# Sums of second-layer weights in the last block pair: held in program order, moved to other places, and split 512 wide

## The chip, the cores and the metric

The kernel runs on one core of a Trainium2 chip. The metric is device time in microseconds, the median of several runs of the whole kernel. A core has five engines with instruction queues of their own: TensorE (PE, matmuls, with PEld for its weight loads), VectorE (DVE), ScalarE (ACT), GpSimd (POOL) and SyncE (SP, which here only issues DMAs). An engine works through its queue in order, so an instruction that waits holds up all that stand behind it.

## The reference: block attention, then a mixture of four experts

```python
def _attn_ref(q, k, v):                  # q, k, v: (4, 8, 768, 64)
    k_sum = max over blocks of 32 keys;  v_sum = mean over blocks of 32
    scores_l = scale * q @ k.T, masked to |i - j| < 16
    scores_s = scale * q @ k_sum.T + log(32)
    a = softmax over [scores_l, scores_s]
    return a @ [v, v_sum]

def _moe_ref(x, domain_probs, w1, w2):   # x: (3072, 512), E = 4, F = 1024
    p = domain_probs / (domain_probs.sum(-1, keepdims=True) + 1e-09)
    for e in range(E):
        h = np.maximum(x @ w1[e], 0.0)
        out += p[:, e:e + 1] * (h @ w2[e])
```

The attention is abridged here to its formulas. Its output, turned to 3072 rows of 512, is the x of the experts. Inputs and output are float32; the kernel carries each operand of a large product as two parts, a high part and the rest (low), and forms three products of them.

## The kernel before: staging, order and the names that matter

The 3072 rows are eight blocks of 384. Block 0 and block 1 and then both together are run through two experts each in float32 parts; the other six blocks are run as three pairs (1, 2, 3 in `PAIRS`, line 928), all four experts for a pair, in float16 parts. Pair 3 takes the experts in the order 3, 2, 1, 0. The attention of later blocks is interleaved with the experts' products of earlier ones; it is done when pair 2 is.

**The products.** In a pair the first product (x with w1, `first`, line 1174) multiplies 2 x 2 blocks with seven block products in place of eight, so it needs sums and differences of the blocks of x and of w1. `SEVEN` (line 1034) lists the seven steps m = 0 to 6: the PSUM bank (a, b, c, d) that a step adds to, and its two operands. Some steps are followed by a copy or a sum from bank to bank: at m = 0 ACT copies a to b, at m = 1 it copies d into a tile called `five`, at m = 2 DVE forms c from b and `five`, at m = 4 it forms d from b and `five`. In the traces the banks of the first product are pha to phd, those of the second poa to pod; `five` is p in the first and q in the second. The banks come from three PSUM pools: a from one of two buffers, d from another of two, b and c from a third of four. In pairs 1 and 2 the second product (h with w2, `second`, line 969) is plain. In pair 3 alone (`SEVENS`, line 929) it is done by seven as well (`second_sevens`, line 1078), for three row tiles t = 0 to 2 one after the other. A step there is 12 matmuls of 256 columns. Pair 3 therefore also needs sums of the blocks of h (`h_operands`, line 1137, on ACT, DVE and POOL behind the first product) and of the blocks of w2.

**The w2 sums.** `w2_operands(e, i)` (line 855) makes one set of them, for i = 0 to 3 of each expert: two raw loads of 256 KB into tiles `wr` (4 buffers, used for all raw weights), two scalings by ACT, then for each of seven 256-wide operands a cast to float16 on ACT (the high part) and a difference on POOL or DVE (the low part), and four differences that make the sums in place in the raw tiles. The result lies in two tiles (`w2g` in the traces): four operands in a tile of tag w2 (8 buffers), three in a tile of tag x (14 buffers, `NX`). The same x slots hold the seven operands of x for the running pair (`x_operands`, line 453) and, earlier, pieces of the attention. Tag chunk (2 buffers) holds raw x and raw pieces of k and v. `fetch7` (line 958) takes the next set off the list `todo7`. It is called four times in the first product of pair 3's first expert (line 1233), for that expert's own sets, and at m = 1 and m = 5 of t = 0 and t = 1 in each `second_sevens` (line 1131), for the next expert's.

**What sets the order.** The program is traced in the order of the Python code; then a scheduler orders each engine's queue by priority (the order of tracing, unless raised) and by when its own timing model takes an operand or a buffer to be ready. An instruction traced late can thus be placed early if its buffers are free. `tc.high_priority(offset=RUSH)` raises bank copies and what follows them (lines 1111 and 1210). The class `Engine` (line 67) can hold an instruction behind the one traced before it on the same engine: `pinned["rest"]` for ACT, DVE, POOL and PE, `pinned["load"]` for SP. Both are on for the first rows and off from lines 1270 and 1275 on, so through all pairs nothing is held. The first operands of w1 in pair 3 come ready made from DRAM into `w1g` (7 buffers, two per set); their loads and the raw loads of w2 share SP's queue.

`with_fetch` (line 982) runs a plain second product unit by unit, and lets `fetch` load w1 operands at units 1 and 8. `pair_units` (line 1039) calls it for the last expert of pairs 1 and 2 (line 1074). That second product yields 17 units: three for each of the three row tiles of the pair's first block, then eight for the second block.

Of the kernel before, what the change touches and what calls it, by code (L numbers as in the profile page):

```python
# [11 lines left out]
F16 = mybir.dt.float16  # L12
AF = mybir.ActivationFunctionType
ALU = mybir.AluOpType
AX = mybir.AxisListType

P = 128
# [12 lines left out]
FC = DF // P  # L30
# [11 lines left out]
CHUNKS = 2  # L42
XFREE = 28
NX = 14
# [18 lines left out]
def attn_moe(ctx: ExitStack, tc: tile.TileContext, qvL, qv0, v0L, kD, kT, vT, w1L, w2L, dpL, cst, out):  # L63
    nc = tc.nc
    pinned = {"load": True, "rest": True}
# [16 lines left out]
    V, A, PL, PE = (Engine(e, "rest") for e in (nc.vector, nc.scalar, nc.gpsimd, nc.tensor))  # L82
# [11 lines left out]
    sb = pool("sb")  # L94
# [754 lines left out]
        return ws  # L849


    TS = ("11", "t1", "t2", "21"), ("t3", "22", "t4")
    w2_sums = {}

    def w2_operands(e, i):
        groups = [
            sb.tile([P, 4, 512], F16, name=f"w2g0{e}_{i}", tag="w2", bufs=FC),
            sb.tile([P, 3, 512], F16, name=f"w2g1{e}_{i}", tag="x", bufs=NX),
        ]
        ws = {w: groups[j][:, n, :] for j, names in enumerate(TS) for n, w in enumerate(names)}  # L860
        r1, r2 = (load_weights(w2L, e, 2 * i + j, "2") for j in range(2))
        for raw in (r1, r2):
            A.mul(raw, raw, scale_w[e][1])
        b11, b12 = r1[:, 0:256], r1[:, 256:512]
        b21, b22 = r2[:, 0:256], r2[:, 256:512]

        def parts(w, raw, lo):
            hi, low = ws[w][:, 0:256], ws[w][:, 256:512]
            A.copy(hi, raw)
            lo.tensor_tensor(low, raw, hi, op=ALU.subtract)  # L870

        parts("11", b11, PL)
        V.tensor_tensor(b11, b12, b11, op=ALU.subtract)
        parts("22", b22, PL)
        V.tensor_tensor(b12, b12, b22, op=ALU.subtract)
        V.tensor_tensor(b22, b22, b11, op=ALU.subtract)
        parts("t1", b11, V)
        parts("21", b21, PL)
        parts("t2", b22, V)
        PL.tensor_tensor(b21, b21, b22, op=ALU.subtract)  # L880
        parts("t3", b12, V)
        parts("t4", b21, PL)
        w2_sums[e, i] = {w: (x[:, 0:256], x[:, 256:512]) for w, x in ws.items()}

    acc, added = {}, {}
    scaled_pw = {}
# [42 lines left out]
    SEVENS = (3,)  # L929
# [3 lines left out]
    es_of = dict(PAIRS)  # L933
# [22 lines left out]
    todo7 = [(e, i) for pr, es in PAIRS if pr in SEVENS for e in es for i in range(FC // 2)]  # L956

    def fetch7():
        if todo7:
            w2_operands(*todo7.pop(0))  # L960

    ready2 = {}

    def fetch2():
        if todo2:
            pr, e, j = todo2.pop(0)
            ready2.setdefault((pr, e), {}).update(w2_scaled(e, j))

    def second(tbs, e, hT, w2, last):
        whole = tbs if last else tbs[:-1]  # L970
        for tb in whole:
            for t in range(TB // P):
                yield from mm2(tb, e, [t], hT, w2)
        for tb in tbs[len(whole) :]:
            yield from mm2(tb, e, range(TB // P), hT, w2)
# [3 lines left out]
            for t in range(TB // P):  # L979
                yield from mm2(tb, e, [t], hT, w2, range(FC))  # L980

    def with_fetch(units, places=()):
        for n, us in enumerate(units):
            if n in (1, 8):
                fetch()
            if n in places:
                fetch2()
            yield us

    def plain_units(tbs, e, early=0, last=False):  # L990
# [48 lines left out]
    def pair_units(pr, es, last=False):  # L1039


        tbs = (2 * pr, 2 * pr + 1)
        if pr in SEVENS:
            for e in es:
                hs = {}
                kept.clear()
                for us in first(pr, tbs, e, hs, None, None):
                    yield us, 1.0
                yield from second_sevens(pr, tbs, e, hs)
            return  # L1050
        behind = None
        for n, e in enumerate(es):
            hT = {}
            w2 = kept.pop(e)[1] if pr > 1 and e in kept else ready2.setdefault((pr, e), {})
            kept.clear()
            units = first(pr, tbs, e, hT, w2, "hl"[n % 2])
            if behind is None:
                for us in units:
                    yield us, SLOW
            else:  # L1060
                todo_us = 0.0
                for us in units:
                    yield us, 1.0
                    todo_us += us * second_share
                    while todo_us > 0.0:
                        us2, _ = next(behind, (todo_us, 0))
                        todo_us -= us2
                        if _:
                            yield us2, 1.0
                yield from behind  # L1070
            if n < len(es) - 1:
                behind = tile_by_tile(tbs, e, hT, w2)
        kept[e] = {}, w2
        yield from with_fetch(second(tbs, e, hT, w2, last))

    second_share = 2 * (TB // P) * FC * 3 * US2 / (2 * FC * 3 * KC * US1 * 7 / 8)

    def second_sevens(pr, tbs, e, hs):
        for t in range(TB // P):
            bank = {}  # L1080

            def new(k):
                room, tag = dict(a=(ps_sc, "sc"), d=(ps_av, "av")).get(k, (ps_mm, "mm"))
                bank[k] = room.tile([P, 512], F32, name=f"po{k}{pr}_{e}_{t}", tag=tag)[:, :256]
                return bank[k]

            gts = [tb * (TB // P) + t for tb in tbs]
            if e == es_of[pr][0]:
                for gt in gts:
                    acc[gt] = sb.tile([P, DM], F32, name=f"acc{gt}", tag="acc", bufs=6)  # L1090

            def add(row, col, k):
                gt = gts[row]
                pe = scaled_pw[e][:, gt % (S // P)]
                to = acc[gt][:, col * 256 : (col + 1) * 256]
                if e == es_of[pr][0]:
                    V.tensor_scalar_mul(to, bank[k], pe)
                else:
                    V.scalar_tensor_tensor(to, bank[k], pe, to, op0=ALU.mult, op1=ALU.add)

            for m, (k, h, w) in enumerate(SEVEN):
                first = m < 2
                o = new(k) if first else bank[k]
                again = dict(skip_group_check=not first)
                for i in range(FC // 2):
                    hh, hl = (x[:, t * P : (t + 1) * P] for x in hs[i, h])
                    wh, wl = w2_sums[e, i][w]
                    PE.matmul(o, hh, wh, start=i == 0 and first, stop=False, **again)
                    PE.matmul(o, hh, wl, start=False, stop=False, **again)
                    PE.matmul(o, hl, wh, start=False, stop=i == FC // 2 - 1, **again)  # L1110
                with tc.high_priority(offset=RUSH):
                    if m == 0:
                        A.copy(new("b"), o)
                    elif m == 1:
                        five = sb.tile([P, 256], F32, name=f"q5{pr}_{e}_{t}", tag="hs", bufs=2)
                        A.copy(five, o)
                    elif m == 2:
                        V.tensor_tensor(new("c"), o, five, op=ALU.add)
                    elif m == 3:
                        add(0, 0, "a")  # L1120
                    elif m == 4:
                        V.tensor_tensor(bank["d"], o, five, op=ALU.add)
                        add(1, 1, "d")
                    elif m == 5:
                        add(0, 1, "c")
                    else:
                        add(1, 0, "b")
                    if e == es_of[pr][-1] and m > 4:
                        gt = gts[m - 5]
                        SP.dma_start(out[gt * P : (gt + 1) * P, :], acc.pop(gt))  # L1130
                if m in (1, 5) and t < 2:
                    fetch7()
                yield 12 * US2 / 2, 1.0
        for i in range(FC // 2):
            w2_sums.pop((e, i))
# [38 lines left out]
    def first(pr, tbs, e, hT, w2, room):  # L1174
        xp = xpair[pr]
        sevens = pr in SEVENS
# [7 lines left out]
        for n, i in enumerate(order):  # L1184
# [14 lines left out]
            for m, (k, w, x) in enumerate(SEVEN):  # L1199
# [29 lines left out]
                else:  # L1229
                    to_h(hT, tbs[0], e, f2, o, room_h)  # L1230
                ahead_of.close()
                if sevens:
                    if e == es_of[pr][0] and (n, m) in ((0, 0), (0, 3), (1, 2), (2, 1)):
                        fetch7()
                elif m == 3:
                    if len(w2) < FC:
                        fetch2()
                yield 6 * US1
# [3 lines left out]
    for n in range(per, NTB * per):  # L1242
        k = n + SHIFT * (n >= 2 * per)
# [11 lines left out]
    for b in range(1, B):  # L1255
        k = 2 * per * b + SHIFT
# [24 lines left out]
    for (tbs, experts), end in zip(plan, ENDS):  # L1281
        pair = tbs if isinstance(tbs, int) else None
        n = 2 if pair else len(tbs)
# [5 lines left out]
        parts, u, done = None, 0.0, 0.0  # L1289
        for e in experts[:1] if pair else experts:  # L1290
            if pair:
                units = pair_units(pair, experts, last=nxt == NTB // 2)
            else:
                units, ahead = ahead or plain_units(tbs, e, last=n == 2 and e == experts[-1]), None
# [77 lines left out]
```

## Time and profile before

| what | us |
|---|---|
| median of 3 runs | 1187.58 |
| lowest and highest run | 1186.81, 1189.34 |
| the profiled execution, its own time | 1185.91 |
| its span, first to last instruction | 1184.0 |
| TensorE busy | 1105.7 |
| VectorE busy | 812.9 |
| ScalarE busy | 693.6 |
| GpSimd busy | 581.0 |

Mean granted TensorE clock over the span is 0.977 of full speed. In the profile every instruction has line 75, that of the helper class, so groups are told apart by engine, operation and tile names: `out<-in`, partitions x elements and type, the count, and behind the bar the busy time in us, the mean duration in ns, and the idle time of the engine just before them with what ended it. A row of the waits is: who waited, for whom, us in total, number of times, the longest.

### The profile page before, as it was taken

What the parts mean: (1) busy time and instruction counts of PE and PEld (TensorE: products, weight loads), DVE (VectorE), ACT (ScalarE), POOL (GpSimd) and SP (SyncE); (2) the same over time, 40 slices, a digit from 0 to 9 for tenths busy, and PEclk for the clock granted to TensorE, in tenths of its full rate; (3) what the DMA queues carried; (4) which work ended last, traced back from release to release, by engine and by line L of the source; (5) the groups of instructions that cost most, each with busy time, mean ns of one, the idle gap of its engine ahead of it and who ended that gap; (6) DMA issues with size and microseconds to landing.
All of it is one profiled execution on the core that took longest, in us unless ns stands there. A gap on an engine that the chain in (4) does not pass through costs nothing.

```text
span 1184.0 us, 20638 instructions
## 1 busy us (share of the span) xinstructions
PE 1105.7 (93%) x6994; PEld 757.4 (64%) x6994; DVE 812.9 (69%) x1959; ACT 693.6 (59%) x1930; POOL 581.0 (49%) x698
## 2 busy tenths in 40 slices
PE   9899698999999879889979999999999999999898
PEld 7888587898897545445545455555555458575767
DVE  5888779875888667676888354445457674958574
ACT  5767466664557788777676344444445662828251
POOL 2587455772736777686554111223214651827251
PEclk9999788999999899999999999999999999999999
DMA  6476756663845768776885453554632340504001
GB/s 237 137 218 168 193 141 184 166 170 94 254 105 150 219 222 260 241 254 206 251 284 144 134 155 127 130 179 133 194 89 67 111 139 23 177 17 161 19 14 54
DMA packets 169305, 184.10 MB, mean 155 GB/s; under 512 B 79344, under 2 KB 115184, under 8 KB 169200
## 3 DMA queue, kind: packets, MB, share of 16 engines
q1 hardware_dynamic: 169200, 182.79, 51.3%
q8 instruction: 55, 0.90, 0.3%
q14 instruction: 50, 0.41, 0.1%
HBM read 131.76 MB, written 34.08 MB: 140 GB/s over the span
## 4 chain that ended last, share of the span: by engine, by line
PE 48%; DVE 19%; DMA 14%; ACT 9%; POOL 5%; issue 4%; SPq 1%; ACTq 0%; POOLq 0%; DVEq 0%
PE po L75 14%; PE ph L75 6%; PE phb L75 6%; PE pha L75 4%; PE pob L75 4%; DMA wr<-in_w1L 4%; DMA wr<-in_w2L 3%; PE psc L75 3%; PE poa L75 2%; PE phd L75 2%; PE phc L75 2%; ACT wr L75 2%; DMA xr<-xd 2%; DVE wr L75 2%; DVE ms L75 2%
## 5 line engine op out<-in xcount | busy, mean ns | idle before, releaser
L75 PEld LDWEIGHTS <-w1g 128*128 128x128 f16 x2016 | 195.7, 99 | 176.8 <-issue 38.3
L75 PE MATMUL po<-w2s,h 128*128 128x512 f16 x1152 | 271.4, 381 | 1.1 <-DVE h L75 1.1
L75 PEld LDWEIGHTS <-h 128*128 128x128 f16 x1584 | 152.1, 98 | 128.1 <-issue 2.6
L75 PE MATMUL phb<-x_t,w1g 128*128 128x384 f16 x864 | 166.4, 328 | 24.5 <-ACT phb L75 10.8
L75 PE MATMUL ph<-xh,w 128*128 128x384 f32 x512 | 144.2, 352 | 9.1 <-ACT xh L75 3.7
L75 POOL TENSOR_TENSOR ks<-kr,ks 128x304 fp32r<-128x304 f32 x112 | 100.2, 899 | 98.9 <-ACT ks L75 98.0
L75 PE MATMUL po<-w,hh 128*128 128x512 f32 x384 | 122.2, 397 | 0.0
L75 PE MATMUL pha<-x,w1g 128*128 128x384 f16 x576 | 115.1, 333 | 6.4 <-DVE nb L75 4.8
L75 ACT ACTIVATE ms<-ms,nb 96x152 f32<-96x152 f32 x256 | 104.2, 414 | 23.7 <-DVE nb L75 23.0
L75 POOL TENSOR_TENSOR v<-qv,v 128x256 f16<-128x256 f32 (+1 forms) x56 | 43.5, 779 | 133.3 <-ACT v L75 125.9
L75 POOL TENSOR_TENSOR w<-wr,w 128x512 fp32r<-128x512 f32 x60 | 81.6, 1368 | 55.3 <-ACT w L75 51.0
L75 PEld LDWEIGHTS ph<-xh,w 128*128 128x128 f32 x512 | 97.7, 197 | 12.0 <-ACT xh L75 4.0
L75 POOL TENSOR_TENSOR w2g<-wr,w2g 128x256 f16<-128x256 f32 x64 | 47.6, 759 | 101.9 <-ACT w2g L75 101.8
L75 DVE CUSTOM_DVE_ANT_0 ms<-psc,c_sb 96x152 f32<-96x152 f32 x256 | 69.3, 305 | 37.9 <-PE psc L75 34.9
L75 PE MATMUL ph<-xl,w 128*128 128x384 f32 x256 | 88.9, 347 | 0.0
L75 PEld LDWEIGHTS po<-w,hh 128*128 128x128 f32 x384 | 70.9, 189 | 14.5
L75 PE MATMUL po<-w,hl 128*128 128x512 f32 x192 | 76.4, 399 | 0.0
L75 ACT CAST aw<-ms 96x512 f16<-96x512 f32 x112 | 49.4, 488 | 42.1 <-issue 21.5
L75 DVE TENSOR_TENSOR aw<-ms,aw 96x512 f16<-96x512 f32 x112 | 68.5, 644 | 7.8 <-ACT aw L75 7.7
L75 PE MATMUL psc<-ks,qs 128*96 128x152 f32 x448 | 63.9, 269 | 6.3 <-POOL qs L75 4.6
L75 ACT CAST w<-wr 128x512 fp32r<-128x512 f32 x84 | 50.9, 616 | 32.1 <-DMA wr<-in_w1L 22.1
L75 POOL TENSOR_TENSOR qs<-qv,qs 64x384 fp32r<-64x384 f32 x56 | 58.7, 1049 | 15.6 <-ACT qs L75 11.8
(184 smaller groups left out, 2259.0 us busy)
## 6 DMA issues: line engine op xcount, KB each, us to landing
wr<-in_w2L SPq DMA_DIRECT2D x104, 256.0 KB, 3.1
wr<-in_w1L SPq DMA_DIRECT2D x76, 256.0 KB, 3.3
qv<-in_qvL SPq DMA_DIRECT2D x56, 320.0 KB, 3.7
kr<-in_kD SPq DMA_DIRECT2D x56, 256.0 KB, 3.2
w1g<-wdg SPq DMA_DIRECT2D x28, 512.0 KB, 3.5
w1g<-wdg SPq DMA_DIRECT2D x28, 384.0 KB, 3.4
wdg<-w1g SPq DMA_DIRECT2D x16, 512.0 KB, 3.9
wd<-w2s SPq DMA_DIRECT2D x16, 512.0 KB, 4.5
```

The lines of the kernel that those rows point to most:

```text
L75: ins = getattr(self.engine, name)(*a, **kw)
```

## The change

Three things are changed, all in the w2 sums of pair 3.

- The four sets of pair 3's first expert are taken in the plain second product of the last expert of pair 2, at its units 0, 3, 6 and 9, and no longer in the first product of pair 3's first expert. The sets of the next expert are taken at (t, m) = (0, 3), (0, 6), (1, 2) and (1, 5) of each `second_sevens`.
- While a set is traced, `pinned["rest"]` is on: each of its ACT, DVE and POOL instructions is held behind the instruction traced before it on its engine. Instructions outside of the set are still placed freely. The loads are not held.
- A set's operands are laid out so that high parts of neighbours lie side by side, and so do low parts. Three of the four pairs of cast and difference are then 512 wide for two operands together, one is 256 wide; all four sums are made by DVE. The set i = 3 of every expert but the first takes its three-operand tile from tag chunk, of the same size, in place of tag x.

```diff
-    TS = ("11", "t1", "t2", "21"), ("t3", "22", "t4")
+    TS = ("21", "22", "t1", "t3"), ("11", "t4", "t2")
-    def w2_operands(e, i):
+    def w2_operands(e, i, tag, bufs):
         groups = [
-            sb.tile([P, 4, 512], F16, name=f"w2g0{e}_{i}", tag="w2", bufs=FC),
-            sb.tile([P, 3, 512], F16, name=f"w2g1{e}_{i}", tag="x", bufs=NX),
+            sb.tile([P, 2, 4, 256], F16, name=f"w2g0{e}_{i}", tag="w2", bufs=FC),
+            sb.tile([P, 2, 3, 256], F16, name=f"w2g1{e}_{i}", tag=tag, bufs=bufs),
         ]
...
-        def parts(w, raw, lo):
-            hi, low = ws[w][:, 0:256], ws[w][:, 256:512]
+        def parts(j, n, count, raw, lo):
+            hi, low = (groups[j][:, k, n : n + count, :].rearrange("p n d -> p (n d)") for k in range(2))
             A.copy(hi, raw)
             lo.tensor_tensor(low, raw, hi, op=ALU.subtract)

-        parts("11", b11, PL)
+        parts(1, 0, 1, b11, PL)
+        parts(0, 0, 2, r2, PL)
         V.tensor_tensor(b11, b12, b11, op=ALU.subtract)
-        parts("22", b22, PL)
         V.tensor_tensor(b12, b12, b22, op=ALU.subtract)
+        parts(0, 2, 2, r1, V)
         V.tensor_tensor(b22, b22, b11, op=ALU.subtract)
-        parts("t1", b11, V)
-        parts("21", b21, PL)
-        parts("t2", b22, V)
-        PL.tensor_tensor(b21, b21, b22, op=ALU.subtract)
-        parts("t3", b12, V)
-        parts("t4", b21, PL)
+        V.tensor_tensor(b21, b21, b22, op=ALU.subtract)
+        parts(1, 1, 2, r2, V)
...
     def fetch7():
         if todo7:
-            w2_operands(*todo7.pop(0))
+            e, i = todo7.pop(0)
+            pinned["rest"] = True
+            w2_operands(e, i, *(("chunk", CHUNKS) if i == 3 and e != es_of[SEVENS[0]][0] else ("x", NX)))
+            pinned["rest"] = False
...
-    def with_fetch(units, places=()):
+    def with_fetch(units, places=(), early7=()):
...
+            if n in early7:
+                fetch7()
...
-        yield from with_fetch(second(tbs, e, hT, w2, last))
+        yield from with_fetch(second(tbs, e, hT, w2, last), early7=(0, 3, 6, 9) if pr + 1 in SEVENS else ())
...
-                if m in (1, 5) and t < 2:
+                if (t, m) in ((0, 3), (0, 6), (1, 2), (1, 5)):
                     fetch7()
...
-                if sevens:
-                    if e == es_of[pr][0] and (n, m) in ((0, 0), (0, 3), (1, 2), (2, 1)):
-                        fetch7()
-                elif m == 3:
+                if m == 3 and not sevens:
                     if len(w2) < FC:
                         fetch2()
```

More of the change, by code (lines that the diff above doesn't have):

```diff
@@ L849, in w1_operands @@
         return ws
-    TS = ("11", "t1", "t2", "21"), ("t3", "22", "t4")
+    TS = ("21", "22", "t1", "t3"), ("11", "t4", "t2")
     w2_sums = {}
-    def w2_operands(e, i):
+    def w2_operands(e, i, tag, bufs):
         groups = [
-            sb.tile([P, 4, 512], F16, name=f"w2g0{e}_{i}", tag="w2", bufs=FC),
-            sb.tile([P, 3, 512], F16, name=f"w2g1{e}_{i}", tag="x", bufs=NX),
-        ]
-        ws = {w: groups[j][:, n, :] for j, names in enumerate(TS) for n, w in enumerate(names)}
+            sb.tile([P, 2, 4, 256], F16, name=f"w2g0{e}_{i}", tag="w2", bufs=FC),
+            sb.tile([P, 2, 3, 256], F16, name=f"w2g1{e}_{i}", tag=tag, bufs=bufs),
+        ]
+        w2_sums[e, i] = {
+            w: (groups[j][:, 0, n, :], groups[j][:, 1, n, :]) for j, names in enumerate(TS) for n, w in enumerate(names)
+        }
         r1, r2 = (load_weights(w2L, e, 2 * i + j, "2") for j in range(2))
@@ L865, in w2_operands @@
         b21, b22 = r2[:, 0:256], r2[:, 256:512]
-        def parts(w, raw, lo):
-            hi, low = ws[w][:, 0:256], ws[w][:, 256:512]
+        def parts(j, n, count, raw, lo):
+            hi, low = (groups[j][:, k, n : n + count, :].rearrange("p n d -> p (n d)") for k in range(2))
             A.copy(hi, raw)
             lo.tensor_tensor(low, raw, hi, op=ALU.subtract)
-        parts("11", b11, PL)
+        parts(1, 0, 1, b11, PL)
+        parts(0, 0, 2, r2, PL)
         V.tensor_tensor(b11, b12, b11, op=ALU.subtract)
-        parts("22", b22, PL)
         V.tensor_tensor(b12, b12, b22, op=ALU.subtract)
+        parts(0, 2, 2, r1, V)
         V.tensor_tensor(b22, b22, b11, op=ALU.subtract)
-        parts("t1", b11, V)
-        parts("21", b21, PL)
-        parts("t2", b22, V)
-        PL.tensor_tensor(b21, b21, b22, op=ALU.subtract)
-        parts("t3", b12, V)
-        parts("t4", b21, PL)
-        w2_sums[e, i] = {w: (x[:, 0:256], x[:, 256:512]) for w, x in ws.items()}
+        V.tensor_tensor(b21, b21, b22, op=ALU.subtract)
+        parts(1, 1, 2, r2, V)
     acc, added = {}, {}
```

## The prediction

> **What bounds the kernel now.** I read the page first, then TensorE's waits from 860 us on, then the busy time by stage.
>
> ```profile
> span 1184.0 us, 20638 instructions
> PE 1105.7 (93%) x6994; PEld 757.4 (64%) x6994; DVE 812.9 (69%) x1959; ACT 693.6 (59%) x1930; POOL 581.0 (49%) x698
> ```
>
> TensorE (PE) is busy for 93% of the span. Its matmuls are the same before and after the change, so only its idle time and its clock can be won. The change touches the last pair, which begins near 941 us; there the waits are:
>
> ```profile
> PE phb L75 <- ACT phb L75: 7.4, 6, 2.0
> PE pod L75 <- DVE hs L75: 4.0, 2, 2.1
> PE phb L75 <- DVE phc L75: 2.2, 3, 0.9
> PE phb L75 <- DVE phd L75: 1.8, 2, 1.2
> ```
>
> The names ph are banks of the first product, po of the second, hs a sum of h blocks. So PE waits almost only for ScalarE (ACT) and VectorE (DVE) to move first-product banks. By stage (window; busy time of PE, PEld, DVE, ACT, POOL; clock; DMA share; GB/s):
>
> ```profile
> 910.00:941.00 31.00, 31.00 (x147) 14.12 (x145) 22.25 (x43) 19.34 (x47) 18.12 (x26) 1.00 0.33 105
> 941.00:970.00 29.00, 25.36 (x145) 14.64 (x144) 19.79 (x35) 18.97 (x44) 15.16 (x17) 0.94 0.42 139
> 976.00:1000.00 24.00, 24.00 (x216) 20.99 (x215) 11.06 (x22) 5.04 (x15) 3.98 (x5) 1.00 0.07 24
> 1014.00:1050.00 36.00, 30.36 (x223) 21.20 (x222) 30.19 (x53) 24.37 (x62) 24.03 (x26) 1.00 0.37 126
> 1050.00:1062.00 12.00, 12.00 (x107) 10.18 (x105) 4.84 (x11) 2.20 (x6) 1.30 (x2) 1.00 0.00 1
> 1072.00:1106.00 34.00, 28.20 (x194) 18.62 (x193) 31.12 (x51) 26.87 (x68) 27.13 (x30) 1.00 0.42 141
> 1106.00:1128.00 22.00, 22.00 (x193) 18.56 (x191) 8.05 (x18) 1.67 (x4) 0.00 (x0) 1.00 0.01 1
> 1128.00:1160.00 32.00, 32.00 (x224) 21.80 (x223) 23.21 (x39) 21.31 (x49) 17.93 (x19) 1.00 0.04 13
> ```
>
> Row 1 is the second product of the pair before; rows 2, 4, 6 and 8 are the first products of the last pair's four experts (3, 2, 1, 0), rows 3, 5 and 7 their second products. PE is idle for 29.00 - 25.36 = 3.64 us under expert 3's first product, 36.00 - 30.36 = 5.64 under expert 2's, 34.00 - 28.20 = 5.80 under expert 1's and 0 under expert 0's. The three with stalls also carry sets of w2 sums (one set is one call of w2_operands) for a later expert; the last carries only one. In row 6 DVE is busy for 31.12 of 34 us; in row 7, the second product right behind, for 8.05 of 22, and ACT for 1.67. So the work sits under the stage that has no room for it, and the next stage is empty. The empty stage cannot take it now: of the 14 x slots, 7 hold the last pair's x operands and 4 the running expert's sums, so three sets of the next expert fit and the fourth waits until the running second product is done.
>
> How a set stops PE is seen in ACT's timeline (start, duration, instruction, idle time and releaser):
>
> ```profile
> 944.11 0.40 ACT L75 CAST w2g<-wr 128x256 f16<-128x256 f32 x1 [0.41 <-DVE wr L75]
> 945.10 0.71 ACT L75 CAST w2g<-wr 128x256 f16<-128x256 f32 x2 [0.59 <-DVE wr L75]
> 946.03 0.40 ACT L75 CAST w2g<-wr 128x256 f16<-128x256 f32 x1 [0.21 <-POOL wr L75]
> 946.34 0.47 ACT L75 COPY phb<-pha 128x384 f32<-128x384 f32 x1
> ...
> 949.49 0.72 ACT L75 ACTIVATE wr<-wr,scalew 128x512 f32<-128x512 f32 x1 [0.87 <-DMA wr<-in_w2L]
> ```
>
> The copy phb<-pha, for which PE waits, stands behind three casts of a set that themselves wait for DVE and GpSimd (POOL). PE's waits for it between 941 and 952 us are:
>
> ```profile
> PE phb L75 <- ACT phb L75: 3.6, 2, 2.0
> ```
>
> That is 1.8 us each. In the same row of the windows the granted clock is 0.94: 0.06 x 29 = 1.74 us more.
>
> **The change part by part.** *First expert's sets in the preceding pair.* Row 1 shows the scheduler already running sets there. What changes is that they are held to four places in that second product, and that the next expert's three sets no longer follow them: those are traced at m = 3 and m = 6 of row tile 0 and m = 2 and m = 5 of row tile 1 of expert 3's second product, and held there. Row 1 has 0 idle time of PE with DVE at 22.25 of 31 us, and it will hold fewer sets than now, so I cost this part at nothing; its cover is a 31 us stage in which PE waits for none of it. Gone is what is queued ahead of phb<-pha at 946 us: 3.64 us, and the clock with it, 1.74.
>
> *The other experts' sets under the running second product.* Each leaves the first product of its own expert. The remaining DVE work there can be read from row 8: with a single set beside it, 23.21 of 32 us and no stall. I take the whole 5.64 and 5.80. Late next in that stage is then nothing that row 8 shows.
>
> *Room.* The fourth set of every expert but the first takes its smaller tile from the chunk tag (2 buffers), which is idle once the x operands are made; so 7 + 4 + 3 = 14 x slots hold two experts, and no set waits for the running product's end. The eight w2 slots hold two experts already.
>
> *The loads.* Each set still issues two raw loads of 256 KB into the four wr buffers; their number is the same. They pass SP, in order, among the w1g loads:
>
> ```profile
> 947.90 0.34 SPq L75 DMA_DIRECT2D wr<-in_w2L  x1
> 949.00 56.33 SPq L75 DMA_DIRECT2D w1g<-wdg  x9
> 1008.70 3.46 SPq L75 DMA_DIRECT2D wr<-in_w2L  x3
> ```
>
> From 949 to 1005 us no raw load is issued: all four wr buffers were full (two sets waiting for slots). With slots free, the first two sets of an expert find their data in place and the other two loads come due when the first two sets are done, ahead of the w1g load that waits for the next first product.
>
> *The shorter chain.* A set goes from 9 ACT, 5 POOL and 6 DVE instructions to 6, 2 and 6 (two scalings and four casts; one 256-wide and one 512-wide POOL difference; four 256-wide and two 512-wide DVE ones). Durations in the last pair, and of 512-wide forms of the same operations earlier in the kernel:
>
> ```profile
> L75 ACT CAST w2g<-wr 128x256 f16<-128x256 f32 x110 | 40.7, 405 | 21.8 <-DVE wr L75 16.3 <-PE poa L75 2.4 <-POOL wr L75 1.6
> L75 ACT ACTIVATE wr<-wr,scalew 128x512 f32<-128x512 f32 x28 | 20.2, 721 | 5.7 <-DMA wr<-in_w2L 4.8 <-POOL w2g L75 0.8
> L75 ACT CAST w2s<-wr 128x512 f16<-128x512 f32 x16 | 9.8, 615 | 0.1
> L75 POOL TENSOR_TENSOR w2g<-wr,w2g 128x256 f16<-128x256 f32 x62 | 46.3, 762 | 93.9 <-ACT w2g L75 93.8
> L75 POOL TENSOR_TENSOR wr<-wr 128x256 f32<-128x256 f32 x16 | 12.9, 806 | 11.6 <-DVE wr L75 11.6
> L75 POOL TENSOR_TENSOR w2s<-wr,w2s 128x512 f16<-128x512 f32 x16 | 20.4, 1276 | 8.8 <-ACT w2s L75 8.7
> L75 DVE TENSOR_TENSOR wr<-wr,wr 128x256 f32<-128x256 f32 x32 | 19.5, 609 | 0.2
> L75 DVE TENSOR_TENSOR w<-wr,w 128x512 fp32r<-128x512 f32 x24 | 20.3, 851 | 1.4 <-ACT w L75 1.4
> ```
>
> Per set, ACT goes from 2 x 0.721 + 7 x 0.405 = 4.28 us to 1.44 + 0.405 + 3 x 0.615 = 3.69; POOL from 4 x 0.762 + 0.806 = 3.85 to 0.762 + 1.276 = 2.04; DVE will take about 4 x 0.609 + 2 x 0.851 = 4.14. Four sets: 14.8, 8.2 and 16.6 us. The length of a second product follows from two of its steps, which begin 1.31 us apart:
>
> ```profile
> 1046.61 1.47 PE L75 MATMUL pob<-w2g,hs 128*128 128x256 f16 x12
> 1047.92 1.47 PE L75 MATMUL poc<-w2g,hs 128*128 128x256 f16 x12
> ```
>
> It has 7 steps x 3 row tiles, 27.5 us. By row 7, DVE does 8.05 / 22 x 27.5 = 10.1 us of its own there, so it would be filled to 26.7 of 27.5 at these mean prices. That is the tight place. A set that slips past the end is covered by row 8, where one set costs nothing.
>
> *The new wait.* Held in order, a cast or a difference of a set can stand waiting at the head of ACT or DVE while something PE needs is queued behind it: the copies pob<-poa and q<-pod, and the sums into banks c and d.
>
> ```profile
> L75 ACT COPY pob<-poa x12: 357/361/377, 977.4 to 1171.2; 128x256 f32<-128x256 f32 x12
> L75 DVE TENSOR_TENSOR wr<-wr,wr x32: 408/424/1134, 906.0 to 1130.9; 128x256 f32<-128x256 f32 x32
> ```
>
> Those have one step of seven (1.31 us) of slack, 0.36 of which the copy takes. No row shows this stage with sets in it. The lower bound is 0 (row 1, with sets and no stall, though there no bank is copied while its product runs); a gain beyond the removed stalls is excluded since PE has no idle time in rows 3, 5 and 7. The upper bound is all 18 copies of the three second products caught at 1.8 us, 32 us. I take one hold of the longest DVE form, 1.13 us, per second product, 3.4 us, near the lower end because the stage has 1 us of slack per copy and rush priority for them.
>
> **Sum.** 3.64 + 5.64 + 5.80 + 1.74 = 16.8 us won, 3.4 given back: 13.4. The profiled execution took 1185.91 us (span 1184.0), so 1172.5; the median of the runs lies 1.67 above it, so 1174.
>
> **Rivals.** *Late data.* If SP commits to the waiting w1g load first, the third and fourth sets of an expert get their raw rows only when the next first product runs. Half of the sets stay where they stall now: half of 5.64 + 5.80 is lost, 5.7 us. Gain 7.7, 1180. For it: the 56 us block above. Against: the raw loads are traced earlier than that w1g load.
>
> *A longer POOL hold.* A 256-wide DVE difference takes 0.41 us at best and 1.13 at worst, 0.72 more, about one POOL operation (0.76). With a 512-wide POOL difference (1.28) the hold is 0.51 longer, once per set; if each of the 12 sets under second products puts that on a sum that PE needs, 6.2 us more is given back: gain 7.2, 1180.4. The Trainium skill, page "SBUF — State Buffer", section "SBUF: two separate sides", states that GpSimd and a DVE operation with two SBUF inputs take a shared port as an exclusive lock for the whole instruction; by that rule wider POOL operations are the wrong direction, and the trace's 1.13 against 0.41 us agrees. Against: POOL's operations per set fall from five to two and its time by almost half.
>
> *ACT held by its order, slower than before.* The mechanism at 946 us moves into the second product: ACT stands at a cast that waits for DVE, with pob<-poa or q<-pod behind. It decides from 16.8 / 1.8 = 9.3 held copies of 18 on. With 14 held: 14 x 1.8 - 16.8 = 8.4 us slower, 1196. For it: DVE near full, and sets that wait for DVE and POOL in turn. Against: the rushed copies are placed by the scheduler, and only the set is held.
>
> *No effect.* If slots or data keep the sets where they run now, the time stays 1187.6.
>
> **How the numbers follow.** Forecast 0.60, late data 0.13, POOL hold 0.08, no effect 0.06, ACT held 0.13. A measurement of this kernel tells 0.2% (2.4 us) from no change. Faster by more: 0.60 + 0.13 + 0.08 = 0.81; within: 0.06; slower: 0.13. The range takes the first three cases, 0.81: from the whole 16.8 us off the lowest run (1186.81 - 16.8 = 1170) to two late sets with the 3.4 doubled (1187.58 - 7.7 + 3.4 = 1183.3, 1184 with the runs' spread).
>
> **What would show it.** Right: no idle time of PE between 941 and 970 us and clock 1.00 there; DVE above 80% in the second products and near 23 us in each first product; raw loads issued during second products; POOL busy there, where it now shows 0.00. Wrong: PE waits for ACT pob, q or DVE poc, pod in second products (ACT held); raw loads only behind the w1g load (late data); POOL differences in front of the DVE sums that PE waits for.

## The result and the profile after

The changed kernel takes 1175.05 us (median of 4 runs, 1173.76 to 1176.73) against 1187.19 for the kernel before (4 runs): a ratio of 0.9896, 95% interval 0.9875 to 0.9916. The forecast was 1174, in a range of 1170 to 1184. The profiled execution took 1173.76 us.

The first lines of the page of the changed kernel:

```profile
span 1172.0 us, 20540 instructions
PE 1101.6 (94%) x6994; PEld 757.0 (65%) x6994; DVE 816.7 (70%) x1959; ACT 694.1 (59%) x1882; POOL 549.3 (47%) x650
```

The matmuls are the same 6994. ACT has 48 instructions fewer and POOL 48 fewer, 3 of each in 16 sets, as counted. The waits of TensorE (PE) in the last pair, from 935 us on (who waits, for whom, us in total, times, longest):

```profile
PE phb L75 <- ACT phb L75: 5.2, 1, 5.2
PE phb L75 <- DVE phc L75: 1.5, 4, 0.6
```

Six kinds of wait became two. One wait of 5.2 us is nearly all that is left, and nothing waits for a bank of the second product. By stage, in windows that answer to those of before (busy us of PE, PEld, DVE, ACT, POOL; clock; DMA share; GB/s):

```profile
908.00:939.00 31.00, 31.00 (x146) 14.10 (x145) 23.07 (x45) 16.27 (x44) 15.53 (x22) 1.00 0.22 70
939.00:968.00 29.00, 23.83 (x137) 13.67 (x136) 21.50 (x37) 17.31 (x37) 11.17 (x11) 0.88 0.48 159
976.00:1000.00 24.00, 24.00 (x216) 20.93 (x214) 18.38 (x37) 13.86 (x29) 7.75 (x8) 1.00 0.22 73
1005.00:1032.00 27.00, 26.74 (x178) 17.18 (x176) 22.91 (x39) 18.67 (x40) 13.85 (x14) 1.00 0.42 137
1032.00:1059.00 27.00, 27.00 (x238) 23.00 (x236) 20.85 (x40) 16.19 (x34) 9.72 (x10) 1.00 0.24 79
1060.00:1088.00 28.00, 27.71 (x185) 17.86 (x183) 23.19 (x40) 19.19 (x41) 14.59 (x15) 1.00 0.42 133
```

The first products of the second and third expert (rows 4 and 6) now leave PE idle for 0.26 and 0.29 us, where it was 5.64 and 5.80; the second expert's second product (row 5) carries 16 us of ACT work and PE still has no idle time in it. The first expert's first product (row 2) got worse: 5.17 us idle in place of 3.64, and a clock of 0.88 in place of 0.94.

To compare kernels the last pair is cut into four stages: from the start of its first matmul (a group pha<-x,w1g) to the start of the last group pob<-w2g,h of the first expert, and from there to the same group of each next expert. The two borders of the first stage are, in PE's timeline of before

```profile
941.20 1.14 PE L75 MATMUL pha<-x,w1g 128*128 128x384 f16 x6
1004.99 1.47 PE L75 MATMUL pob<-w2g,h 128*128 128x256 f16 x12
```

and of the changed kernel

```profile
939.13 1.14 PE L75 MATMUL pha<-x,w1g 128*128 128x384 f16 x6
1004.42 1.47 PE L75 MATMUL pob<-w2g,h 128*128 128x256 f16 x12
```

that is 63.79 and 65.29 us. All kernels of this study, read in the same way (ratio to the kernel before on the same chip):

| kernel | expert 1 | 2 | 3 | 4 | sum | median us | ratio, 95% interval |
|---|---|---|---|---|---|---|---|
| before | 63.79 | 61.62 | 61.54 | 50.75 | 237.70 | 1187.19 | 1 |
| changed | 65.29 | 55.22 | 55.52 | 51.53 | 227.56 | 1175.05 | 0.9896 (0.9875 to 0.9916) |
| one_unit_later | 58.14 | 55.03 | 55.23 | 51.53 | 219.93 | 1170.68 | 0.9839 (0.9800 to 0.9877) |
| not_held | 60.21 | 66.13 | 60.37 | 50.75 | 237.46 | 1189.76 | 0.9999 (0.9976 to 1.0022) |
| narrow_splits | 68.64 | 55.42 | 55.70 | 50.42 | 230.18 | 1180.32 | 0.9924 (0.9896 to 0.9952) |
| chunk_tile_only | 63.58 | 59.87 | 56.90 | 50.75 | 231.10 | 1181.81 | 0.9938 (0.9906 to 0.9970) |
| no_chunk_tile | 66.48 | 56.54 | 56.46 | 52.28 | 231.76 | 1180.30 | 0.9927 (0.9898 to 0.9955) |
| wide_splits_only | 59.10 | 64.05 | 64.55 | 51.78 | 239.48 | 1191.06 | 1.0027 (1.0004 to 1.0049) |
| all_on_dve | 61.12 | 54.81 | 54.81 | 50.74 | 221.48 | 1172.48 | 0.9859 (0.9823 to 0.9895) |
| first_expert_own_product | 66.81 | 55.10 | 55.95 | 51.52 | 229.38 | 1180.13 | 0.9935 (0.9912 to 0.9957) |
| hold_only | 66.94 | 56.09 | 56.02 | 51.53 | 230.58 | 1181.05 | 0.9915 (0.9890 to 0.9940) |
| first_sets_free | 58.15 | 54.81 | 55.41 | 51.53 | 219.90 | 1172.42 | 0.9844 (0.9821 to 0.9866) |
| later_and_all_on_dve | 58.20 | 54.81 | 54.81 | 50.75 | 218.57 | 1170.07 | 0.9835 (0.9805 to 0.9865) |

The changed kernel wins 6.40 + 6.02 us in the second and third stage and loses 1.50 + 0.78 in the first and fourth: 10.14 of the 12.0 us by which the span is shorter. Of the rest, 2.07 us lie ahead of the last pair (941.20 against 939.13), which varies by more than that between the profiles of these kernels (939.13 to 950.85); the time after the last border is 0.2 us longer.

### The profile page after: what moved, and what is told of

Its sections match the earlier page's. It is cut to its first block, busy times and chain, and to the rows that moved or that the text cites. A ratio compares the mean times of both kernels' runs of the same rounds, so it can differ in the third digit from the quotient of the medians.

```text
span 1172.0 us, 20540 instructions
## 1 busy us (share of the span) xinstructions
PE 1101.6 (94%) x6994; PEld 757.0 (65%) x6994; DVE 816.7 (70%) x1959; ACT 694.1 (59%) x1882; POOL 549.3 (47%) x650
## 4 chain that ended last, share of the span: by engine, by line
PE 34%; DVE 9%; DMA 3%; ACT 3%; issue 2%; POOL 1%; SPq 0%; POOLq 0%; DVEq 0%; ACTq 0%
PE po L75 11%; PE phb L75 8%; PE pha L75 5%; PE phc L75 2%; DVE wr L75 2%; PE phd L75 2%; PE poa L75 1%; PE pob L75 1%; PE psc L75 1%; ACT wr L75 1%; DVE acc L75 1%; POOL w2g L75 1%; DVE xr L75 1%; DMA vch<-in_vT 1%; PE px L75 1%
## 5 line engine op out<-in xcount | busy, mean ns | idle before, releaser
L75 POOL TENSOR_TENSOR w2g<-wr,w2g 128x256 f16<-128x256 f32 (+1 forms) x32 | 29.9, 951 | 99.6 <-ACT w2g L75 99.3
L75 ACT CAST ks<-kr 128x304 fp32r<-128x304 f32 x112 | 48.2, 443 | 42.8 <-PE psc L75 41.9
```

What stands on the lines that cost most here:

```text
L75: ins = getattr(self.engine, name)(*a, **kw)
```

## The experiments

**What made the gain: the hold, the slot or the splits?** My theory: the gain is where the sets run, and the hold keeps them there. The rivals: the shorter chain of a set, or the freed slot.

*not_held* takes the hold away and leaves the rest.

```diff
-            pinned["rest"] = True
             w2_operands(e, i, *(("chunk", CHUNKS) if i == 3 and e != es_of[SEVENS[0]][0] else ("x", NX)))
-            pinned["rest"] = False
```

> The changed kernel without the hold: places, chunk tile and 512-wide splits stay, the scheduler may move the sets. Theory (where the sets run makes the gain, and only the hold keeps them there): sets of later experts go back under first products, PE waits there for several us again as before, and the time is 1182 to 1188 us. Rival (shorter chain or the free slot makes the gain): 1174 to 1177.

It is no faster than the kernel before (0.9999), a little slower even than expected. The casts of the sets tell where they run. In the second expert's stage, ACT's casts into w2g in the first product and in the second (busy us, count) are, in the kernel before:

```profile
1005.00:1039.00 34.00, 9.38 (x25) 1.00 0.50 170
1039.00:1066.00 27.00, 1.11 (x3) 1.00 0.00 1
```

in the changed kernel:

```profile
1005.00:1032.00 27.00, 0.62 (x1) 1.00 0.42 137
1032.00:1059.00 27.00, 7.46 (x15) 1.00 0.24 79
```

and in not_held:

```profile
1006.00:1044.00 38.00, 7.99 (x15) 0.96 0.44 140
1044.00:1071.00 27.00, 1.66 (x3) 1.00 0.05 19
```

With slot and splits but no hold, 15 of 18 casts stand under the first product again, and the stage is 66.13 us long. Called under the second product, they are placed by the scheduler under the next first one.

*hold_only* is the other way about: the kernel before, with the hold and nothing else.

```diff
+            pinned["rest"] = True
             w2_operands(*todo7.pop(0))
+            pinned["rest"] = False
```

> The kernel before with the hold alone: old places (the first expert's sets in its own first product), tag x, 256-wide splits. Theory (the hold does most of it): second and third stage 56 to 57 us in place of 61.6, because three of four sets now run in the second product; the first stage grows to 66 us or more; 1177 to 1183 us. Rival (the hold needs the chunk tile or the short chain with it): second and third stage 59 us or more, 1184 or more.

The second and third stage fall to 56.09 and 56.02 us, 22 of 28 casts now under the second product:

```profile
1009.00:1037.00 28.00, 2.22 (x6) 1.00 0.40 132
1037.00:1064.00 27.00, 7.78 (x22) 1.00 0.25 79
```

So the hold alone brings 5.5 us in each of the two stages, of the 6.4 and 6.0 of the whole change. In the first stage, where the first expert's own sets are held under its first product, it costs 3.15 us.

*chunk_tile_only* gives the kernel before the chunk tile, *wide_splits_only* the 512-wide splits (layout and order as in the diff above, in tag x, free).

```diff
-            w2_operands(*todo7.pop(0))
+            e, i = todo7.pop(0)
+            w2_operands(e, i, *(("chunk", CHUNKS) if i == 3 and e != es_of[SEVENS[0]][0] else ("x", NX)))
```

> The kernel before with one thing changed: the fourth set of experts 2, 1 and 0 takes its smaller tile from tag chunk. Theory: with the slot free and nothing held, the scheduler still gathers sets under first products: 1184 to 1188 us. Rival (the missing slot was what kept the sets out of the second products): 1174 to 1178.

Here I was wrong: the slot alone is worth 6.6 us in the last pair. In the second stage 9 casts stand under the second product, in place of 3, with nothing held:

```profile
1005.00:1036.00 31.00, 8.19 (x23) 1.00 0.53 172
1036.00:1063.00 27.00, 3.28 (x9) 1.00 0.08 28
```

The third stage is left with 18 casts under its first product, in place of 25, and is 4.64 us shorter. The scheduler uses the room if it has a slot, but only in part.

> The kernel before with the 512-wide splits alone; no hold, old places, tag x. Theory: the sets stay under first products, a little shorter (ACT 0.6 us and POOL 1.8 us less per set), so half a stall at best: 1182 to 1187 us. Rival (ACT and POOL time of the sets was what filled the first products): 1178 or less.

Also off: no gain but a small loss, with stages of 64.05 and 64.55 us. The first stage is 4.7 us shorter than before: ACT's casts of the sets take 1.12 us of its first product (942 to 970 us) in place of 3.63, so shorter chains do help there. In the later stages PE waits 14 times, 14.0 us in all, against 11 times and 11.4 us before. Why the scheduler's order there is worse was not followed up.

*narrow_splits* and *no_chunk_tile* take one part out of the changed kernel: its 256-wide splits are those of before in one, the fourth set takes tag x in the other.

```diff
-            w2_operands(e, i, *(("chunk", CHUNKS) if i == 3 and e != es_of[SEVENS[0]][0] else ("x", NX)))
+            w2_operands(e, i, "x", NX)
```

> The changed kernel with the 256-wide splits of the kernel before (9 ACT, 5 POOL, 6 DVE instructions per set); hold, places and chunk tile stay. Theory: second products have room for the longer chain, so at most 1 to 3 us are lost: 1175 to 1178 us. Rival (the shorter chain makes the gain, DVE and ACT being nearly full in the second products): PE waits in second products, 1182 or more.

> The changed kernel with the fourth set of every expert back in tag x; hold, places and splits stay. The fourth set must then wait for the end of the running second product. Theory (the hold keeps three sets in the second product, and one set under a first product costs nothing, as for the last expert of the kernel before): stages of 55 to 56 us for the second and third expert and 1174 to 1178 us. Rival (the slot itself is worth what the chunk tile alone gained, some 6 us): stages of 58 us or more, 1179 to 1183.

Both end 2 us above the 1178 us that was expected at most; for no_chunk_tile that is a time of the rival's, but its stages are not. In narrow_splits it is the first stage that is longer, by 3.35 us (68.64 against 65.29); in the second and third the cost is 0.2 us each, with two waits of about 0.3 us in each for sums of the second product, the new wait of the prediction in small. With the chunk tile missing, every stage is 0.8 to 1.3 us longer. So neither is the source of the 6 us, and one set under a first product costs about 1 us, not nothing. Where the chain's length does count is the first stage.

**Why the first expert's stage got longer.** The timeline of ACT in the changed kernel:

```profile
942.47 0.62 ACT L75 CAST w2g<-wr 128x512 f16<-128x512 f32 x1 [1.64 <-DVE wr L75]
942.99 1.39 ACT L75 ACTIVATE wr<-wr,scalew 128x512 f32<-128x512 f32 x2
944.29 0.91 ACT L75 CAST w2g<-wr 128x256 f16<-128x256 f32 x2
947.31 0.62 ACT L75 CAST w2g<-wr 128x512 f16<-128x512 f32 x1 [2.11 <-DVE wr L75]
947.84 0.47 ACT L75 COPY phb<-pha 128x384 f32<-128x384 f32 x1
```

The third and fourth set still run when the first product has begun at 939 us, and phb<-pha stands behind them: the same mechanism as before at 946 us. They are late together with the x operands. The first casts of x parts in ACT's timeline stand, in the kernel before, at

```profile
821.26 0.60 ACT L75 CAST x<-xr 128x192 f16<-128x192 f32 x2 [3.71 <-DMA xr<-xd]
```

and in the changed kernel at

```profile
910.37 1.11 ACT L75 CAST x<-xr 128x192 f16<-128x192 f32 x4
```

so that all four parts share 910 to 935 us with the sets: between 908 and 939 us the instructions on xr, the raw x, take 14.47 us of DVE and 8.15 of ACT. At unit 0 the first set is traced just ahead of the x operands, whose seven tiles come from the same tag x. Two kernels test this.

```diff
-  early7=(0, 3, 6, 9) if pr + 1 in SEVENS else ()
+  early7=(1, 4, 7, 10) if pr + 1 in SEVENS else ()      # one_unit_later
...
-            pinned["rest"] = True
+            pinned["rest"] = e != es_of[SEVENS[0]][0]       # first_sets_free
```

> The first expert's four sets are called at units 1, 4, 7 and 10 of the preceding second product, in place of 0, 3, 6 and 9; nothing else differs from the changed kernel. Theory: at unit 0 the first set's tile of tag x is traced ahead of the seven tiles of the x operands, so these get no slot until the pair before releases its own, all parts of x are made at 910 us and later in place of 821 to 912, and the sets are pushed into the first product, where ACT stands at a cast of the fourth set with phb<-pha behind it (5.17 us of waiting, clock 0.58 in one 8 us window). One unit later the x tiles come first: parts of x from about 820 us on, no wait of phb over 1 us near 941 to 952, clock 1.00, and a time of 1167 to 1170 us. Rival: the four held sets are simply too long for that stage whatever the slots: the wait stays at 4 to 6 us and the time at 1174 to 1176.

> The changed kernel with the first expert's four sets free and all others held. The trace order is as in the changed kernel, so the first set's x tile still comes ahead of the x operands, but the set can run early and does not keep the order of the slots waiting. Theory (the held first set keeps the x tiles from their slots): the parts of x come earlier than 910 us in part, the wait of 5.17 us is gone or below 2 us, the first stage is 58 to 61 us, 1168 to 1173 us. Rival (the order of the slots alone does it, held or not): first stage 64 us or more, 1175 or more.

In one_unit_later the x parts begin at

```profile
824.46 0.60 ACT L75 CAST x<-xr 128x192 f16<-128x192 f32 x2 [3.56 <-DMA xr<-xd]
```

all 16 casts of the first expert's sets are done before its first product,

```profile
890.00:944.00 54.00, 8.62 (x16) 1.00 0.24 72
944.00:975.00 31.00, 0.00 (x0) 1.00 0.38 127
```

and the stage is 58.14 us, 7.15 less. The first set's first cast stands at 898.61 us in place of 910.08, and in the last 31.69 us before the pair (913 to 944.69) the instructions on xr take 2.62 us of DVE and 1.41 of ACT. The time, 1170.68, lies just above the 1167 to 1170 expected. In first_sets_free the x parts begin at 824 us as well, and the stage is 58.15. So the late x parts come from both together, a set that is traced ahead of the x operands and is held. That they then wait for slots of tag x is read from the code; no run shows the queue for slots by itself.

*first_expert_own_product* calls the first expert's sets, held, where the kernel before had them.

```diff
-  early7=(0, 3, 6, 9) if pr + 1 in SEVENS else ()
+  early7=()
...
+                if sevens:
+                    if e == es_of[pr][0] and (n, m) in ((0, 0), (0, 3), (1, 2), (2, 1)):
+                        fetch7()
-                if m == 3 and not sevens:
+                elif m == 3:
```

> The changed kernel with the first expert's sets called in its own first product, where the kernel before had them, but held; the rest as changed. Theory: four held sets of about 7 us do not fit beside h_operands in a 27 us first product: several us of waits of PE for phb or phc, the first expert's stage 65 us or more and a time of 1173 to 1180, no better than the changed kernel, against 58 us for the sets one unit later in the preceding pair. Rival (the place does not matter as long as the x parts keep their slots): a stage of 58 to 60 us, 1168 to 1172.

66.81 us, as expected: held sets do need another place than their own first product, and the preceding pair is the right one if they are called one unit later. The time, 1180.13, lies at the upper end of the 1173 to 1180 expected.

**Is DVE full in the second products?** *all_on_dve* gives DVE the two low parts that POOL had.

```diff
-        parts(1, 0, 1, b11, PL)
-        parts(0, 0, 2, r2, PL)
+        parts(1, 0, 1, b11, V)
+        parts(0, 0, 2, r2, V)
```

> The changed kernel with all low parts of the sets on DVE, none on POOL: about 1.1 us more DVE work per set, 4.4 per expert, and no POOL instruction of a set that could hold DVE up. Theory of the prediction (DVE nearly full in second products, 26.7 of 27.5 us): PE waits of 3 us or more per expert, 1180 us or more. Rival (DVE has room there, since its sums run at their uncontended 0.42 and 0.69 us): stages within 1 us of the changed kernel's 55.2 and 55.5, 1173 to 1178.

The theory that DVE is nearly full there falls. The second and third stage are 54.81 us, shorter than the changed kernel's, with no wait of PE in them; the times alone do not tell the two kernels apart (0.9859 and 0.9896, with intervals that overlap). The differences between two raw blocks (wr<-wr,wr; count, least, median and greatest ns) show why, in the changed kernel:

```profile
L75 DVE TENSOR_TENSOR wr<-wr,wr x32: 407/418/1370, 912.1 to 1116.0; 128x256 f32<-128x256 f32 x32
L75 POOL TENSOR_TENSOR w2g<-wr,w2g x32: 670/968/1366, 910.6 to 1112.8; 128x256 f16<-128x256 f32 x16, 128x512 f16<-128x512 f32 x16
```

and in all_on_dve:

```profile
L75 DVE TENSOR_TENSOR wr<-wr,wr x32: 410/416/424, 918.6 to 1115.5; 128x256 f32<-128x256 f32 x32
```

With POOL out of the sets no such difference takes over 0.424 us; with it, one takes up to 1.370. POOL's median of 0.968 mixes two shapes: its 256-wide differences take 0.67 to 0.78 us, the 512-wide ones 1.15 to 1.37. In the changed kernel each DVE difference of over 1 us between raw blocks began while a 512-wide one of POOL ran, and ended about 0.28 us after it. In all_on_dve the other form, wr<-wr, still reaches 1.17 us three times in 32, each time at a POOL instruction of other work, on h:

```profile
1005.61 0.91 POOL L75 TENSOR_TENSOR h<-r,h 128x384 f16<-128x384 f32 x1 [27.46 <-ACT h L75]
1005.63 1.16 DVE L75 TENSOR_TENSOR wr<-wr 128x256 f32<-128x256 f32 x1
```

The Trainium skill's page "SBUF — State Buffer", section "SBUF: two separate sides", which has the shared port held for a whole instruction, agrees with this. POOL costs in a second way: DVE stands idle until POOL has read a raw block that one of DVE's sums overwrites. Both are seen in DVE's sums of the second expert's second product (count, busy us, mean ns, idle us before), in the changed kernel (1032.14 to 1059.64 us)

```profile
L75 DVE TENSOR_TENSOR wr<-wr 128x256 f32<-128x256 f32 x7 | 5.0, 712 | 3.2 <-POOL w2g L75 3.2
L75 DVE TENSOR_TENSOR wr<-wr,wr 128x256 f32<-128x256 f32 x7 | 4.0, 589 | 0.1
```

and in all_on_dve (1031.6 to 1059.1 us):

```profile
L75 DVE TENSOR_TENSOR wr<-wr 128x256 f32<-128x256 f32 x7 | 2.9, 413 | 0.0
L75 DVE TENSOR_TENSOR wr<-wr,wr 128x256 f32<-128x256 f32 x7 | 2.8, 413 | 0.0
```

So 4.4 us more of work for DVE per expert made it busy for only 1.45 us more of this second product (22.46 against 21.01 us). Without POOL in the sets these two stages are 0.4 and 0.7 us shorter, the first and fourth 4.2 and 0.8; how much of that each of the two ways brings is not separated.

**Both together.** *later_and_all_on_dve* joins the two edits.

> Both edits that made the changed kernel faster: the first expert's sets one unit later, and all low parts of the sets on DVE. If the two gains lie in different places (the first expert's stage; the 0.4 and 0.7 us per later stage that POOL cost), they add: no PE wait over 0.5 us in the last pair, stages of about 58, 54.8, 54.8 and 50.7 us and 1167 to 1170 us. Rival (they overlap, since both shorten the first expert's chain): no better than 1170 to 1172.

The waits of PE in the last pair shrink to one line:

```profile
PE phb L75 <- DVE phc L75: 0.4, 1, 0.4
```

It is the fastest kernel by its last pair, 218.57 us against 227.56 of the changed kernel and 237.70 of the one before. Its ratio, 0.9835, lies below the changed kernel's 0.9896; from one_unit_later's 0.9839 the times do not tell it apart. The stages are as expected; the time, 1170.07, lies where the two expected ranges meet. The gains do not add in full: 7.63 us (one_unit_later) and 6.08 (all_on_dve) of the last pair give 8.99 together. All_on_dve's 4.2 us in the first expert's stage bring nothing more there (58.20 us, 58.14 in one_unit_later), its 1.90 us in the other three are kept.

## Why the prediction was right, and where it was not

- **What binds.** Right: PE's waits for first-product banks were what could be won, and the second products had the room.
- **Second and third expert.** 5.64 and 5.80 us were expected from the stalls; the stages are 6.40 and 6.02 shorter.
- **First expert.** This step failed: "I cost this part at nothing", with 3.64 us and the clock's 1.74 to be won. The stage became 1.50 us longer, an error of 6.9 us, and the sign named for it, no idle time and a clock of 1.00 from 941 to 970 us, did not come (5.17 us idle and 0.88 from 939 to 968). I read from the profile that the stage ahead has room, and not what else the held sets are traced ahead of there: the x operands, with which they share a tag. Moved by one unit, the step gives 5.65 us against the kernel before, about what was predicted.
- **Fourth expert.** Not in the sum: 0.78 us lost, with a wait of 0.62 us for DVE at its start that all_on_dve does not have.
- **Room of DVE.** Mis-sized: I filled the second products to 26.7 of 27.5 us (97%), and above 80% was to be a sign. The second expert's shows 21.01 of 27.5 (76%). The price of a set was not far off, 2 x 0.71 + 2 x 0.59 + 2 x 0.69 = 3.98 us by its means there, in place of 4.14. But only 21 of the 24 DVE instructions of four sets fall in it (12.69 us, in place of 16.6), and DVE's own work there is 8.3 us, in place of 10.1.
- **The new wait.** 3.4 us were given back in the sum; no wait of PE for a bank of the second product is listed. The longer POOL hold that a rival named is there, DVE differences of 1.37 us where the longest was 1.13, but in place of its 6.2 us, stages two to four are only 1.90 us shorter when POOL is out of the sets. The hold of ACT by its order, which the rival took for the second products, stays where it was, in the first expert's first product.
- **Loads.** Right: raw loads are issued during second products (seven from 985.48 us on), not behind the waiting w1g load.

So it was luck that the total came out within about a microsecond. An error of 6.9 us in the first stage and 0.8 in the fourth stood against 3.4 us of waits that did not come, 1 us more in the middle stages, and 2.07 us ahead of the last pair that the change cannot be shown to have made.

## What to carry to other kernels

Where a scheduler places instructions, it is not enough to free room in an empty stage: here the work went there in full only when it was held behind what was traced before it. A held instruction also holds its buffer's turn, so look at what is traced just behind it and draws on the same buffers. And price an operation with the neighbours it will have: DVE's sums took 0.65 us on average beside POOL's differences and 0.41 without them.

## What the runs showed of the hardware beside that

- The time up to the last pair, in which the programs differ little, ran from 939.13 us (the changed kernel, mean clock 0.978) to 950.85 (later_and_all_on_dve, 0.972) in single profiles. By an estimate from span and mean clock, 1172 x 0.022 = 26 us against 1174 x 0.028 = 33 us were lost to the clock; the 7 us between them are over half of that spread. Stages of the trace tell kernels apart that their times cannot.
- After the 5.17 us wait six matmuls took 2.08 us from first to last, against 1.14 elsewhere, and the clock of the 8 us window from 944 us was 0.58. In the kernel before, two waits of 1.60 and 2.04 us close together were followed by six matmuls that took 2.13 us and a clock of 0.83 in the window from 952 us, while after the 2.12 us wait that ended at 1041 us the clock stayed at 1.00.
